# Attention in front of a feed-forward block: scores and sums in row tiles, one transpose a pair, masks added by VectorE, and another order of the first chunk

## The chip, the core and the metric

The kernel runs on one core of one Trainium2 chip. The metric is the device time of one execution in microseconds (us). The core's engines, as the profile calls them, are TensorE (PE; its weight loads PEld), VectorE (DVE), ScalarE (ACT), GpSimd (POOL) and SyncE (SP), which here only issues DMAs. Each engine works through its own queue in program order.

## The reference

Attention over 8 batches of 8 heads, 576 positions, 64 elements a head, with one of two masks, and a feed-forward block on its output. Cut to what matters:

```python
scores = (1 / np.sqrt(64)) * np.matmul(q, k.transpose(0, 1, 3, 2))
rel = pos[:, None] - pos[None, :]
mask_local = (rel >= 0) & (rel < 32)
mask_strided = (rel >= 0) & (pos[None, :] % 32 == pos[:, None] % 32)
# heads 0-3 take mask_local, heads 4-7 mask_strided; the rest is -1e9
attn = np.exp(scores - np.max(scores, axis=-1, keepdims=True))
attn = attn / (np.sum(attn, axis=-1, keepdims=True) + 1e-09)
x = np.matmul(attn, v)                      # regrouped: 4608 tokens x 512
h = x @ w_in                                # 512 x 2048
g = np.maximum(h, 0.0) + np.log1p(np.exp(-np.abs(h)))
out = g @ w_out                             # 2048 x 512
```

All of it is f32. A query of a local head sees only the 32 keys up to its own. For strided heads the host sorts positions by their remainder, so that a query sees only keys of its own group of 18; both masks then need no more than a window of 64 keys for a block of 32 queries.

## The kernel before, in words

**Pairs and blocks.** Heads go in pairs, 4 pairs a batch, 32 in all; pair n is of batch n // 4, and the two heads of a pair fill the 128 partitions of q and k (64 each). The 18 blocks of 32 queries of a pair are held as 9 chunks at two places, so that scores fill 128 partitions (place, head, query) and 9 x 64 columns.

**Scores** (`scores`, L355): q is laid out by `lay_out_q` (L264) as blocks of 64 columns, both heads side by side, with the other head's half of the rows set to zero (`zeros`, L222). One matmul of 128 rows by 64 columns then gives both heads of one block: 18 a pair, alternately for the upper and the lower 64 partitions of the output. In batches 0 and 1 TensorE also adds the mask, through an identity matrix (L340); from batch 2 on VectorE does (`add_mask`, L416).

**Softmax.** Maxima, either a subtraction with one wide exponential or nine exponentials with a bias, sums, `guard`, reciprocal, `normalize` (L389 to L447). In batches 0 and 1 these go by parts of six and three chunks straight from PSUM, from batch 2 on by whole rows of 576 columns (`row_maxima` L421, `row_subtract` L425, `row_exp` L431, `row_sums` L435).

**Transpose.** The probabilities must be turned for the sums: in batch 0 by TensorE against an identity (`early_transposes`, L477, L495) with copies out of PSUM (`early_copy`), later by 16 VectorE transposes of 32 partitions (`prob_transposes`, L457).

**Sums** (`weighted`, L525): 12 matmuls a pair, 128 keys by 64 columns of v, 96 queries each, in two halves of six; `v` is loaded in overlapping pieces (L293, L300). `x_part` splits the result into a high part (ScalarE, L563) and a low part (VectorE, L561).

**Feed-forward.** Tokens go in 9 chunks of 512, the hidden units in 16 blocks f. `hidden` (L629) has 12 matmuls of 512 columns a block, `output` (L669) 12; in between the softplus on ScalarE (L641 to L646) and VectorE (L650), and the split into high and low part (L264, L662). The weights come as 64-bit numbers and are turned into high and low parts in `w_scaled`, `w_shift` (L593), `w_last` (L600), `w_high`, `w_low` (L615).

**Order.** Batches 0 and 1 and chunk 0 follow the table `FIRST`, written out by hand; `ON_POOL`, `ON_VECTOR` and `ON_SCALAR` say which engine takes a step. In it `S` are scores, `X` maxima, `E` exponentials, `M` normalization, `P` or `T` transposes, `V` sums, `H` and `L` the parts of x, `F` and `O` hidden and output blocks (`Fa` is all but the last quarter of one). Everything later is placed by `Plan`, a list scheduler with costs per step: each pair's scores go between two blocks, in one group with the sums of the pair before (`work`, the joint group), one pair for every four steps of F and O.

## Time and profile before

| what | value |
|---|---|
| three runs | 891.38, 892.63, 892.89 us (median 892.63) |
| span of the profiled execution, first to last instruction | 890.1 us |
| DVE, ACT, POOL busy in the first 20 us | 15.2, 14.8, 14.0 us |
| transposes on VectorE (448) | 137 us busy |
| q's layout on ScalarE from pair 4 on (56 copies) | 71 us busy |

The profile is of one execution. A time of its own isn't given for that one; its span is 2.5 us below the median of the runs, for what lies before the first and behind the last instruction. A row of a group reads: line, engine, operation, output <- input, partitions x elements, count, then busy us and mean ns of one, then idle time of the engine just before. Matmuls overlap, so their means are longer than the distance from one to the next; a distance is read from starts in the timeline.

### The profile page before, as it was taken

The numbers are of one execution on the slowest core, as the hardware profiler recorded it, in microseconds if no ns is written. First come the engines' busy times: TensorE is split into PE (matmuls) and PEld (weight loads), VectorE is DVE, ScalarE is ACT, GpSimd is POOL, SyncE is SP. The second block draws the span as 40 slices with busy tenths as digits, with TensorE's granted clock in tenths as the row PEclk, the third lists the DMA queues.
The fourth block names the chain that finished last, engine by engine and source line by source line (L and its number), as shares of the span: only waits on it lengthen the run. The fifth ranks groups of instructions, "written<-read, shape, count | busy, mean of one in ns | idle before, by whom it ended". The sixth has DMA issues, their size and how long they took to land.

```text
span 890.1 us, 14332 instructions
## 1 busy us (share of the span) xinstructions
PE 879.0 (99%) x5634; PEld 723.6 (81%) x5634; DVE 576.6 (65%) x1268; ACT 445.8 (50%) x796; POOL 64.0 (7%) x93
## 2 busy tenths in 40 slices
PE   7999999999999999999999999999999999999998
PEld 5778888888888888888888888888888888888886
DVE  7878877788766777776766676677777333333332
ACT  7999665554544445445445454445543333333332
POOL 7254350000000000000000000000000000000000
PEclk9999999999999999999999999999999999999999
DMA  9856202121211122111211121111200010001001
GB/s 337 314 205 209 93 18 76 56 75 45 91 37 30 36 74 62 44 45 32 92 44 45 44 92 30 30 43 54 81 18 18 1 48 1 0 1 48 1 1 48
DMA packets 50083, 58.27 MB, mean 65 GB/s; under 512 B 3168, under 2 KB 35296, under 8 KB 50016
## 3 DMA queue, kind: packets, MB, share of 16 engines
q1 hardware_dynamic: 49728, 57.03, 19.5%
q8 instruction: 44, 0.72, 0.3%
q10 hardware_dynamic: 288, 0.33, 0.1%
q14 instruction: 23, 0.19, 0.1%
HBM read 47.91 MB, written 9.44 MB: 64 GB/s over the span
## 4 chain that ended last, share of the span: by engine, by line
PE 96%; ACT 2%; DMA 1%; DVE 1%; issue 0%; ACTq 0%
PE py L669 44%; PE ph L629 44%; PE ps L355 3%; PE pv L525 2%; PE po L525 1%; PE po L355 1%; DMA kT<-in_qk_dram 1%; PE idle L692 0%; ACT early_l L399 0%; ACT early_h L264 0%; ACT a_i L589 0%; ACT x_h L563 0%; ACT early_l L264 0%; PE py L355 0%; PE ps L340 0%
## 5 line engine op out<-in xcount | busy, mean ns | idle before, releaser
L669 PE MATMUL py<-w_o,gh 128*128 128x512 f32 x1152 | 358.4, 392 | 0.0
L629 PE MATMUL ph<-x_h,w_i 128*128 128x512 f32 x1152 | 355.5, 390 | 0.0
L641 ACT ACTIVATE u<-ph 128x512 f32<-128x512 f32 x144 | 86.3, 599 | 399.0 <-PE ph L629 398.6
L629 PEld LDWEIGHTS ph<-x_h,w_i 128*128 128x128 f32 x1152 | 215.7, 188 | 45.2
L669 PEld LDWEIGHTS py<-w_o,gh 128*128 128x128 f32 x1152 | 213.9, 188 | 46.4
L669 PE MATMUL py<-w_o,gl 128*128 128x512 f32 x576 | 224.1, 389 | 0.0
L629 PE MATMUL ph<-x_l,w_i 128*128 128x512 f32 x576 | 224.1, 389 | 0.0
L650 DVE SCALAR_TENSOR_TENSOR u<-ph,u 128x512 f32<-128x512 f32 x144 | 99.3, 690 | 178.3 <-ACT u L646 176.3
L457 DVE STREAM_TRANSPOSE pt<-prob 32x192 f32<-32x192 f32 x448 | 137.1, 314 | 6.4
L669 PEld LDWEIGHTS py<-w_o,gl 128*128 128x128 f32 x576 | 108.1, 188 | 22.8
L629 PEld LDWEIGHTS ph<-x_l,w_i 128*128 128x128 f32 x576 | 108.2, 188 | 22.6
L662 DVE TENSOR_TENSOR gl<-u,gh 128x512 fp32r<-128x512 f32 x136 | 94.3, 694 | 12.8 <-ACT gh L264 2.2
L644 ACT ACTIVATE u<-u 128x512 f32<-128x512 f32 x144 | 91.3, 634 | 4.3
L646 ACT ACTIVATE u<-u 128x512 f32<-128x512 f32 x144 | 91.1, 633 | 4.4
L264 ACT COPY qT<-prob 64x576 f32<-64x576 f32 x56 | 70.6, 1261 | 0.3
L264 DVE CAST gh<-u 128x512 fp32r<-128x512 f32 x128 | 54.5, 426 | 10.9 <-DVE u L650 0.5
L416 DVE TENSOR_TENSOR prob<-ps,mask_b 128x384 f32<-128x384 f32 x24 | 13.4, 558 | 50.0 <-PE ps L355 50.0
L355 PEld LDWEIGHTS ps<-kT,qT 128*64 128x64 f32 x720 | 24.0, 137 | 9.0 <-issue 8.5
L355 PE MATMUL ps<-kT,qT 128*64 128x64 f32 x720 | 27.6, 225 | 0.3 <-DMA kT<-in_qk_dram 0.3
L561 DVE TENSOR_TENSOR x_l<-pv,x_h 128x288 fp32r<-128x288 f32 (+2 forms) x47 | 18.8, 412 | 9.0 <-ACT x_h L563 8.9
L447 DVE TENSOR_TENSOR prob<-prob,st 128x576 f32<-128x576 f32 x27 | 21.9, 811 | 0.9
L525 PE MATMUL pv<-pt,v_in 128*64 128x96 f32 x396 | 22.1, 248 | 0.0
(100 smaller groups left out, 481.7 us busy)
## 6 DMA issues: line engine op xcount, KB each, us to landing
v_in<-in_v_dram SPq DMA_DIRECT2D x28, 320.0 KB, 3.5
out_dram<-o SPq DMA_DIRECT2D x35, 256.0 KB, 2.2
ri<-in_moe_w_in_dram SPq DMA_DIRECT2D x16, 512.0 KB, 7.3
ro<-in_moe_w_out_dram SPq DMA_DIRECT2D x16, 512.0 KB, 7.7
kT<-in_qk_dram SPq DMA_DIRECT2D x28, 288.0 KB, 2.9
prob<-in_qk_dram SPq DMA_DIRECT2D x28, 288.0 KB, 2.7
v_in<-in_v_dram SPq DMA_DIRECT2D x28, 48.0 KB, 2.7
room<-in_v_dram SPq DMA_DIRECT2D x4, 320.0 KB, 6.6
```

The source lines that it names most:

```text
L264: (engine.copy if engine is nc.scalar else engine.tensor_copy)(dst, src)
L355: nc.tensor.matmul(ps[rows[place], 64 * (x - lo) : 64 * (x - lo) + 64], lhsT=blocks_of(n)[:, c // 32].rearrange("p h l -> p (h l)"), rhs=k ...
L447: engine.tensor_tensor(pv, pv, rc.unsqueeze(2).broadcast_to(pv.shape), op=ALU.mult)
L457: nc.vector.transpose(pt[32 * (i + c) : 32 * (i + c) + 32, h, a : a + hi - lo, 32 * i : 32 * i + 32,], src[:, lo:hi, 32 * c : 32 * c + 32],)
L525: nc.tensor.matmul(po[64 * h : 64 * h + 64, TILE * x : TILE * x + TILE], lhsT=vs[n][:, a, h, :], rhs=pt_of(n, a)[:, h, a % 2], start=True, ...
L629: nc.tensor.matmul(ph, lhsT=w32["i", f][:, half, cc * P : (cc + 1) * P], rhs=x_of(x, cc)[:, t0 : t0 + n], start=(i == 0), stop=(i == 3 * N ...
L641: nc.scalar.activation(us[c, f], phs[c, f], AF.Abs)
L644: nc.scalar.activation(u, u, AF.Exp, scale=-1.0)
L646: nc.scalar.activation(u, u, AF.Ln, bias=1.0)
L650: nc.vector.scalar_tensor_tensor(u, in0=phs.pop((c, f)), scalar=0.0, in1=u, op0=ALU.max, op1=ALU.add)
L662: engine.tensor_tensor(g, us.pop((c, f)), ghs[c, f].bitcast(F32), op=ALU.subtract)
L669: nc.tensor.matmul(py[t], lhsT=g[:, sl], rhs=w32["o", f][:, half], start=(f == 0 and n == 0), stop=(f == NFC - 1 and n == 2),)
```

## The change

Seven things change together.

1. **Scores** become 36 matmuls a pair: 64 rows (one head), 32 columns of q, 64 keys. Head h and half `half` of the blocks write 32 partitions each. q needs no zeros and one copy for both heads.
2. **The blocks** are numbered in halves: chunk x of half 0 is block x, of half 1 block 9 + x.
3. **Masks** are added by VectorE in all batches; softmax goes by whole rows everywhere. The strided mask is held in full (15 x 64 columns instead of 12 x 64), loaded in three DMAs on SP's queue instead of one on ScalarE's.
4. **Transpose**: one VectorE transpose of 128 x 576, block by block, for each pair, in batch 0 too. The TensorE transposes, their copies, identities and cleared pads are gone.
5. **Sums** become 38 matmuls a pair: 32 keys (rows) of one head and half, 64 columns of v, 64 queries (32 at the ends), each result added up from two neighbouring windows. Half 0 goes to one PSUM bank, half 1 to another, alternately.
6. **v** comes in four loads a pair, one for each half and head, instead of two for both heads.
7. **The table `FIRST`** is a new one, with batch 1's sums in one group with the next scores (`J`), and with other steps on GpSimd and VectorE. In `Plan` the costs of S, Q and P are other numbers.

```diff
 def scores(n, part):
...
-        for x in range(lo, hi):
-            for place in range(2):
-                a, i = block_at(x, place)
-                c = TILE * a + 32 * i
-                nc.tensor.matmul(
-                    ps[rows[place], 64 * (x - lo) : 64 * (x - lo) + 64],
-                    lhsT=blocks_of(n)[:, c // 32].rearrange("p h l -> p (h l)"),
-                    rhs=k_of(n)[:, c : c + 64],
-                    start=not masked or n == 0 and x == lo,
-                    stop=not masked or n > 0 and x == hi - 1,
-                )
+        for x in range(lo, hi):
+            for half in range(2):
+                for h in range(2):
+                    c = 32 * (NCHK * half + x)
+                    to = 64 * half + 32 * h
+                    nc.tensor.matmul(
+                        ps[to : to + 32, 64 * (x - lo) : 64 * (x - lo) + 64],
+                        lhsT=q_of(n)[64 * h : 64 * h + 64, c : c + 32],
+                        rhs=k_of(n)[64 * h : 64 * h + 64, c : c + 64],
+                        start=True,
+                        stop=True,
+                    )
...
+    def prob_transposes(n):
+        nc.vector.transpose(pt_of(n), flat_prob(n))
+
+    def weighted(n, joint=False):
+
+        if joint:
+            banks = shared[n + 1], ps_h.tile([P, 512], F32, tag="ph", name=f"pv_{n}")
+        elif n == 1:
+            banks = [ps_h.tile([P, 512], F32, tag="ph", name=f"pv_{n}_{i}") for i in range(2)]
+        else:
+            taken.append(n)
+            banks = (
+                ps_o.tile([P, 512], F32, tag="po", name=f"pv_{n}_0"),
+                ps_s.tile([P, 512], F32, tag="ps", name=f"pv_{n}_1"),
             )
+        pos[n, 0], pos[n, 1] = banks
+        for j in [*range(1, NCHK + 1, 2), *range(0, NCHK + 1, 2)]:
+            lo, hi = max(j - 1, 0), min(j + 1, NCHK)
+            first = 64 * j - 32 if j else 0
+            for half in range(2):
+                if half == 0 and j == 0:
+                    continue
+                for h in range(2):
+                    at = 64 * half + 32 * h
                     nc.tensor.matmul(
+                        banks[half][64 * h : 64 * h + 64, 32 * lo : 32 * hi],
+                        lhsT=vs[n][at : at + 32, j],
+                        rhs=pt_of(n)[at : at + 32, first : first + 32 * (hi - lo)],
+                        start=(j == 1),
+                        stop=(j == NCHK - 1),
+                        skip_group_check=True,
                     )
...
+    def lay_out_q(n, engine=nc.scalar):
+
+        to = q_of(n).rearrange("p (m l) -> p m l", l=32)
+        copy_on(engine, to, raws[n].rearrange("p (l m) -> p m l", l=32))
...
+        for half in range(2):
+            j = 1 - half
+            for h in range(2):
+                part = src[(HALF - 32) * half : HALF + HALF * half, h * D : h * D + D]
+                rows = slice(64 * half + 32 * h, 64 * half + 32 * h + 32)
+                nc.sync.dma_start(t[rows, j:], part.rearrange("(j k) d -> k j d", k=32))
...
 ON_POOL = """
-D10 D20 x10 D31 hi0 x21 r2 x31 r3 hi3 hi1 ho1 Gh0 ho2 x41 hi4 r4 x50 x51 x60 Gh6 x61 r6 ho8 ho10
+D0 s0 s1 D3 r0 r1 s3 hi4 hi3 ho4 s4 ho5 Gh5 r4 ho2 Gh2 s5 ho9 hi11 hi10 hi14 hi13 Gh6 Gh10 s7 hi15
...
-WIDE = """
-00 11 20 30
+ROWS = """
+0 2
 """.split()
...
-        cost = 1.3
+        cost = 0.8
         if joint(i):
-            cost = 2.5
+            cost = 1.6
```

**TensorE, a joint group.** On TensorE, between the hidden block of one step and the output block of another, a pair's joint group stood like this in the steady stage before (`ps` and `po` take scores, `po` and `pv` sums; a matmul's size is rows of output by columns):

```order
L629 MATMUL ph_10_3077<-x_l_612,w_i_930 128x512
L355 MATMUL ps_0_3094<-kT_101,qT 64x64 x12
L355 MATMUL po_3107<-kT_101,qT 64x64 x6
L525 MATMUL po_3107<-pt,v_in 64x96 x6
L525 MATMUL pv_3120<-pt,v_in 64x96 x6
L669 MATMUL py_104<-w_o_1313,gh_8_3056 128x512 x2
```

In the changed kernel the beginning of the same group, and the first of its sums:

```order
L495 MATMUL ph_11_2433<-x_l_607,w_i_1302 128x512
L297 MATMUL ps_0_2450<-kT_101,qT 32x64 x24
L297 MATMUL po_2475<-kT_101,qT 32x64 x12
L390 MATMUL po_2475<-pt,v_in 64x64 x2
L390 MATMUL pv_2488<-pt,v_in 64x64 x2
L390 MATMUL po_2475<-pt,v_in 64x64 x2
L390 MATMUL pv_2488<-pt,v_in 64x64 x2
```

The place of the group is the same; inside it 18 score matmuls are now 36 and 12 sums 38, and the two banks of the sums alternate, so that neither half is complete before the end.

**VectorE, the start.** On VectorE the softmax of the first two pairs stood so before (`early_l_91` and `early_l_93` hold the probabilities of pairs 0 and 1, `st` their maxima and sums, `py` the scores in PSUM):

```order
L389 TENSOR_REDUCE st_181<-py_104 128x6
L376 TENSOR_TENSOR early_l_91<-py_104,st_181 128x6x64
L389 TENSOR_REDUCE st_181<-py_105 128x3
L393 TENSOR_SCALAR st_181<-st_181 128x3
L385 TENSOR_REDUCE st_181<-early_l_91 128x6
L389 TENSOR_REDUCE st_209<-py_107 128x3
```

And in the changed kernel, up to the third pair's first mask:

```order
L316 TENSOR_TENSOR early_l_93<-py_107,mask_b 128x192
L321 TENSOR_REDUCE st_244<-early_l_93 128x9
L316 TENSOR_TENSOR early_l_95<-py_105,mask_b 128x192
L459 TENSOR_SCALAR a_i_251<-a_i_251 128x512
L316 TENSOR_TENSOR early_l_95<-py_104,mask_b 128x384
L352 TENSOR_REDUCE st_158<-early_l_91 128x9
L321 TENSOR_REDUCE st_249<-early_l_95 128x9
```

VectorE's queue now has two mask additions and one reduction over nine chunks for each pair where it had reductions by parts; the subtraction of pair 0 and all normalizations of batch 0 have gone to GpSimd's queue.

**SP, the loads.** SP's queue for the same time; before, from the first v on (`room` takes v, `early_l` k, `ri` a block of the first weights):

```order
L293 DMA room_109<-in_v_dram 96x128
L300 DMA room_109<-in_v_dram 128x5x128
L282 DMA early_l_97<-in_qk_dram 128x576
L569 DMA ri_368<-in_moe_w_in_dram 128x4x128
L569 DMA ri_394<-in_moe_w_in_dram 128x4x128
L293 DMA room_110<-in_v_dram 96x128
```

And now:

```order
L256 DMA room_109<-in_v_dram 32x9x64 x2
L256 DMA room_109<-in_v_dram 32x10x64 x2
L243 DMA early_l_97<-in_qk_dram 128x576
L435 DMA ri_281<-in_moe_w_in_dram 128x4x128
L435 DMA ri_284<-in_moe_w_in_dram 128x4x128
L256 DMA room_108<-in_v_dram 32x9x64 x2
```

Each v takes four issues; four blocks of the first weights are asked for ahead of the last v, and a first block of the second weights (`ro`) only behind it.

380 lines of the change are left out of this document (112 added, 268 removed).

## The prediction

> **What bounds the kernel now.** The page comes first: its busy shares and its chain.
>
> ```profile
> span 890.1 us, 14332 instructions
> PE 879.0 (99%) x5634; PEld 723.6 (81%) x5634; DVE 576.6 (65%) x1268; ACT 445.8 (50%) x796; POOL 64.0 (7%) x93
> ```
>
> TensorE (PE) is busy 99% of the span, the next engine 65%. So an edit counts by what it does to TensorE's queue, or to the time at which that queue can start. The windows show where TensorE isn't full: I cut the span at the first feed-forward matmul (30.44), at the first score group after chunk 0 (139.66) and at the last sums (697.07).
>
> ```profile
> 0.00:30.44 30.44, 23.49 (x482) 18.29 (x483) 24.21 (x52) 24.39 (x67) 19.18 (x46) 1.00 0.90 309
> 30.44:139.66 109.22, 108.97 (x679) 87.44 (x677) 86.10 (x186) 89.39 (x205) 44.86 (x47) 1.00 0.46 158
> 139.66:697.07 557.41, 557.41 (x3625) 461.50 (x3625) 400.43 (x920) 264.38 (x414) 0.00 (x0) 1.00 0.16 51
> ```
>
> Columns: length, then busy time of PE, PEld, DVE, ACT, POOL, then clock, DMA share, GB/s. Only the front has gaps on TensorE; there VectorE, ScalarE (24 of 30 us each) and the loads (share 0.90) are near full. From 30.44 on nothing but TensorE's own work counts. How much of that is attention, not feed-forward, follows from the dense matmuls, L629 (first two rows) and L669.
>
> ```profile
> 30.44:139.66 109.22, 55.46 (x228) 42.25 (x228) 1.00 0.46 158
> 139.66:697.07 557.41, 265.15 (x1105) 207.28 (x1104) 1.00 0.16 51
> 30.44:139.66 109.22, 46.83 (x192) 35.66 (x192) 1.00 0.46 158
> 139.66:697.07 557.41, 268.32 (x1104) 205.41 (x1104) 1.00 0.16 51
> ```
>
> From the chain of waits, the price of one dense matmul; from the windows, four steps with one pair in them:
>
> ```profile
> 280.75 2.72 PE py L669 x12
> ```
>
> ```profile
> 264.21:288.38 24.17, 24.17 (x158) 20.02 (x157) 16.73 (x38) 11.24 (x18) 0.00 (x0) 1.00 0.14 41
> ```
>
> 12 in 2.72 us are 0.2267 us each. Chunk 0's stage: 420 x 0.2267 = 95.2, so 14.0 of its 109.2 us are the attention of batch 1. Steady stage: four steps are 8 x 2.72 = 21.76, so a **joint group** (scores of one pair, sums of the pair before) costs 24.17 - 21.76 = 2.41 us; 23 of them and one score group alone fill what the 2209 dense matmuls leave of 557.4. The timeline shows one from inside.
>
> ```profile
> 285.81 0.39 PE L629 MATMUL ph<-x_l,w_i 128*128 128x512 f32 x1
> 286.12 0.92 PE L355 MATMUL ps<-kT,qT 128*64 128x64 f32 x24
> 286.87 0.52 PE L355 MATMUL po<-kT,qT 128*64 128x64 f32 x12
> 287.22 0.67 PE L525 MATMUL po<-pt,v_in 128*64 128x96 f32 x12
> 287.72 0.67 PE L525 MATMUL pv<-pt,v_in 128*64 128x96 f32 x12
> 288.31 0.73 PE L669 MATMUL py<-w_o,gh 128*128 128x512 f32 x2
> ```
>
> A matmul on plain f32 leaves two records here (24 for 12 in the program), its two passes. 12 score passes take 287.22 - 286.87 = 0.35, so two take 58 ns; 12 sums passes take 0.50, so two take 83 ns. Scores are 18 x 58 = 1.05 us, sums 12 x 83 = 1.00. The last dense matmul is through at 285.81 + 0.23 = 286.04; 1.05 later would be 287.09, but the sums start at 287.22: **entering** the small tiles costs 0.13. The rest, 2.41 - 2.05 - 0.13 = 0.23, is spent on **leaving** them.
>
> Do two small tiles really run side by side? Batch 0's mask matmuls say so:
>
> ```profile
> 6.57 0.48 PE L355 MATMUL py<-early_l,early_h 128*64 128x64 f32 x6
> 6.88 0.33 PE L340 MATMUL py<-mask_b,ident_b 128*64 128x384 bf16 x2
> 7.04 0.34 PE L355 MATMUL py<-early_l,early_h 128*64 128x64 f32 x6
> ```
>
> Two of 384 columns are through in 0.16 us, and one alone, at the dense rate, needs 384/512 x 0.227 = 0.17. So two column tiles overlap fully. Two f32 passes in 58 ns then mean 58 ns per tile.
>
> **Steady stage, 23 joint groups.** The change makes 36 score matmuls of 32 rows of output on four tiles and 38 sums on four tiles: 148 passes for 60. If four tiles overlap as two do, a tile has 18 score passes, 18 x 58 = 1.05 as before. In the sums the busiest tile has 20 passes: 16 of 64 columns, 16 x 58 = 0.93, and four of 32 columns, at between 29 and 58, taken at 44: 0.17. Together 1.10 for 1.00. Scores and sums no longer have one tile shape, so a change of shape is added between them; the trace has none between two small shapes, so between 0 and 0.23, taken at the entering 0.13, to which it is most alike. That gives 0.23 a group, **+5.3 us** (ends +1 and +9). The Trainium skill, "TensorEngine Tiling (Array Packing)", Tiling Modes, says that any change of tiling mode drains TensorE; by it the addition would be due, and the 0.23 at 285.81 and 288.31 agrees for the shapes that this trace has.
>
> The transposes, q's layout and the masks of later batches cost nothing on this path:
>
> ```profile
> L457 DVE STREAM_TRANSPOSE pt<-prob 32x192 f32<-32x192 f32 x224 | 82.8, 370 | 3.9
> L416 DVE TENSOR_TENSOR prob<-ps,mask_b 128x384 f32<-128x384 f32 x24 | 13.4, 558 | 50.0 <-PE ps L355 50.0
> L416 DVE TENSOR_TENSOR prob<-po,mask_b 128x192 f32<-128x192 f32 x24 | 8.6, 358 | 19.3 <-ACT x_h L563 19.3
> L425 DVE TENSOR_TENSOR prob<-prob,st 128x576 f32<-128x576 f32 x24 | 18.0, 750 | 0.0
> L421 DVE TENSOR_REDUCE st<-prob 128x9 f32<-128x576 f32 x24 | 17.9, 745 | 0.0
> L447 DVE TENSOR_TENSOR prob<-prob,st 128x576 f32<-128x576 f32 x27 | 21.9, 811 | 0.9
> ```
>
> 16 transposes of 32 rows become one of 128 x 576; three of 192 columns would be 1.1 us, the other passes over 576 columns are 0.75 to 0.81, and I take 0.8. VectorE loses some 4 us a pair, but it is idle 28% of that stage and TensorE not at all. This is hidden already; it buys nothing.
>
> **Chunk 0's stage.** Gone are four mask matmuls a pair and the separate score and sum groups; left are a score group (2.15 - 1.10 + 0.36 = 1.41), three joint ones (2.15 + 0.49 = 2.64) and one sums group (1.10 + 0.36 = 1.46): 10.8 for 14.0, **-3.2 us** (-5 to 0). What is late next there is ScalarE, busy 89 of 109 us; it loses a half of q's layout per pair.
>
> **The front.** Batch 0 loses its mask matmuls, the TensorE transposes and their twelve copies; it gains two mask additions a pair and puts two of the four layouts of q, a subtraction and all normalizations on GpSimd. Its end now:
>
> ```profile
> 29.79 0.72 PE L525 MATMUL pv<-early_l,room 128*64 128x96 f32 x12 [0.50 <-DVE x_l L561]
> 30.44 0.73 PE L629 MATMUL ph<-x_h,w_i 128*128 128x512 f32 x2
> ```
>
> F0, the first feed-forward block, needs all four pairs and ends at 30.44 + 2.9 = 33.3. Rows for the new chain:
>
> ```profile
> L431 ACT ACTIVATE prob<-prob 128x576 f32<-128x576 f32 x24 | 16.5, 688 | 9.2 <-DVE prob L425 9.1
> L561 DVE TENSOR_TENSOR x_l<-pv,x_h 128x288 fp32r<-128x288 f32 x35 | 15.7, 451 | 9.0 <-ACT x_h L563 8.9
> L563 ACT CAST x_h<-pv 128x288 fp32r<-128x288 f32 x35 | 13.8, 398 | 8.7 <-PE pv L525 8.6
> L600 DVE SCALAR_TENSOR_TENSOR a_i<-ri,a_i 128x512 uint32<-128x512 uint32 x16 | 11.2, 705 | 0.2
> L264 POOL COPY early_h<-raw_q 64x576 f32<-64x576 f32 x3 | 3.7, 1239 | 0.7 <-DMA raw_q<-in_qk_dram 0.7
> L447 POOL TENSOR_TENSOR early_l<-early_l,st 128x576 f32<-128x576 f32 x2 | 2.6, 1308 | 1.4 <-DVE st L443 1.2 <-ACT early_l L264 0.2
> ```
>
> ```profile
> 9.71 0.31 ACT L399 ACTIVATE early_l<-py,st 128x64 f32<-128x64 f32 x1 [0.75 <-DVE st L393]
> 10.02 0.30 ACT L399 ACTIVATE early_l<-py,st 128x64 f32<-128x64 f32 x1
> ```
>
> Nine exponentials follow each other every 0.3 us: 2.7 a pair. Laying each engine's new queue out with these, 0.1 us between engines: pair 0's q is laid out by 5.7, masked by 8.0, its maxima done at 8.7, subtracted on GpSimd until 10.0, exponentials until 10.7. ScalarE goes on with pair 1's (13.4), pair 2's (15.2, after VectorE's subtraction at 14.4), weights, pair 3's (16.4 to 19.0). GpSimd normalizes four times, 1.3 each, the last until 22.1; VectorE transposes pairs 2, 1 and 3 until 23.3; TensorE's last sums end at 25.3, their high parts at 26.1, the low parts, behind three weight steps on VectorE, at 28.0. F0 ends at 28.7 instead of 33.3: **-4.6 us** (-8 to 0). What is late next is GpSimd's row of normalizations and the loads:
>
> ```profile
> raw_q<-in_qk_dram SPq DMA_DIRECT2D x4, 288.0 KB, 4.8
> room<-in_v_dram SPq DMA_DIRECT2D x4, 320.0 KB, 6.6
> ```
>
> Each v is now four loads instead of two, and up to pair 3's v the queue holds 8 x 288 KB of q and k, one more q, four weights of 512 KB, four v and the masks: 6.3 MB, 20.3 us at 309 GB/s and then some to land, against sums of pair 3 at 24.
>
> **Sum**: -4.6 - 3.2 + 5.3 + 0.1 (two more sums groups' passes at the very end) = -2.4 against the profiled execution, whose span is 890.1. The three runs' median is 892.63, 2.5 above the span for what lies around it; so 892.6 - 2.4 = **890.2**.
>
> **Rivals.** (a) *Four tiles don't overlap.* Head 0 and head 1 sit in different row tiles and write the same bank. If tiles of different rows take turns there, scores and sums double: (1.05 + 1.10) x 27 pairs = +58, **948**: slower. The trace has only tiles with all rows, so nothing speaks on it; the two column tiles that overlapped in one bank speak against. The Trainium skill, "TensorEngine Tiling (Array Packing)", Restrictions and Gotchas, says that different row tiles cannot use one PSUM bank at the same time, which is this rival; no run here shows it yet.
>
> (b) *TensorE can't be fed so fast.* 60 passes in 2.19 us, 36 ns each, is what the trace keeps up over a group; 148 in 2.15 would be 15 ns. At 25, half way, a group has 3.7 us: +1.55 x 27 = +42, **932**. It ends slower than before from 16 ns on. The Trainium skill, "TensorE: Matmul & The Clock Gate", "Wait — 56ns, not 53.3ns?", has a floor of about 25 ns from the start of one matmul to that of the next, which would be about this price; the trace, with two passes of different tiles in 58 ns, stays above that floor and cannot tell.
>
> (c) *Row tiles make a pass cheaper.* A dense pass does 64 columns in 28 ns, a bf16 pair too; only two f32 passes side by side take 58. If that is their common reading of 128 rows at 4 bytes, the sums, whose tiles share no row, halve: -0.55 x 27 = -15, **875**; the scores as well: **861**. For it: all three rates fit. Against: two passes per matmul fit as well with f32 itself at half rate.
>
> (d) *The front doesn't shorten*, held by loads or by GpSimd: -2.4 + 4.6, **895**, from 4 us of delay on.
>
> **How the numbers follow.** Forecast 0.44, (a) 0.09, (b) 0.10, (c) 0.24, (d) 0.13. The forecast's own range is 884 to 897. The range of 862 to 912 leaves out (a), most of (b) and the end of (c), about 0.2. This kernel's measurement can tell about 0.2%, 1.8 us. Faster: 0.26 of the forecast, (c) 0.24, (d) 0.04, 0.54. Same: 0.10 + 0.06 = 0.16. Slower: 0.08 + 0.09 + 0.10 + 0.03 = 0.30.
>
> **What would show it.** In the timeline of a joint group: score passes in 1.05 us and sums in 1.1 (right), 2.1 each (a), an even spacing of all passes above 15 ns (b), 0.55 (c); a gap of some 0.13 between the two. F0 complete near 28.7; the dense matmuls of chunk 0's stage plus 10.8 us. I am wrong if the period of four steps isn't near 24.40, or if TensorE has idle time after F0.

## The result, and where the time went

The changed kernel takes 917.2 us (median of 4 runs, 915.97 to 918.57), the kernel before 892.0 in the same comparison (890.47 to 892.89): a ratio of 1.0284, with a 95% interval of 1.0267 to 1.0301. It is slower by 25 us, where 2.4 us less was forecast, and it lies above the forecast's whole range of 862 to 912. The profiled execution has a span of 914.2 us for 890.1.

The page of the changed kernel, its first lines, then from its list of queues (packets, MB, share of 16 engines) the one that brings instructions:

```profile
span 914.2 us, 19113 instructions
PE 896.8 (98%) x8202; PEld 730.0 (80%) x8202; DVE 473.2 (52%) x863; ACT 401.4 (44%) x748; POOL 52.0 (6%) x62
q8 instruction: 64, 1.05, 0.5%
```

VectorE and ScalarE lost work (577 to 473, 446 to 401 us), VectorE some 4 us a pair as forecast, and TensorE is as full as it was. So the 24 us must be found on TensorE's queue. The windows of the changed kernel, cut at the same events as in the prediction (first feed-forward matmul, first score group after chunk 0, last sums), and the four steps of one joint group; the columns are those of the prediction's windows:

```profile
0.00:36.30 36.30, 22.43 (x602) 18.17 (x603) 20.34 (x42) 18.64 (x57) 13.19 (x24) 0.67 0.90 244
36.30:144.16 107.86, 107.86 (x1013) 87.54 (x1012) 85.75 (x152) 79.13 (x191) 38.86 (x38) 1.00 0.51 159
144.16:717.48 573.32, 573.31 (x5686) 467.32 (x5685) 301.44 (x560) 236.30 (x391) 0.00 (x0) 1.00 0.17 47
717.48:914.20 196.72, 193.18 (x905) 156.92 (x904) 65.72 (x110) 67.35 (x111) 0.00 (x0) 1.00 0.05 17
269.81:294.67 24.86, 24.86 (x245) 20.27 (x244) 12.61 (x23) 10.01 (x16) 0.00 (x0) 1.00 0.15 38
```

Against the stages of before (30.44, 109.22, 557.41, and 890.1 - 697.07 = 193.0) that is +5.9, -1.4, +15.9 and +3.7, together +24.1. The last of these is the strange one: once the last sums are done there is no attention left, only the same 828 feed-forward matmuls, and the stage costs 3.7 us more. The chain of waits shows it at every block. Before, and after, far from any attention:

```profile
736.63 2.72 PE py L669 x12
739.35 2.72 PE ph L629 x12
```

```profile
741.24 2.80 PE py L535 x12
744.04 2.76 PE ph L495 x12
```

Twelve dense matmuls take 2.72 us before, whichever block it is, far from small tiles; after the change mostly 2.76 in a hidden block and 2.80 in an output block. There are 144 of each: 144 x (0.04 + 0.08) = 17 us by these rounded rows; by the starts of the matmuls themselves (2.758 and 2.796) it is 16.4. That takes the usual block for every block. Added up one by one, the distances from each dense matmul behind F0, the first feed-forward block, to the next matmul on TensorE are 802.1 us here and 787.7 in e1 below, where the price is the old one: the term is 14.4 us. The granted clock is 1.00 in both, and the instructions are the same. Nothing in the forecast's sum had this term: it took the 0.2267 us of a dense matmul as given.

The other surprise is the front, which grew from 30.44 to 36.30 us. Its granted clock is 0.67 where it was 1.00, and its loads ran at 244 GB/s where it was 309. The joint groups, which the prediction feared most, look like this in the timeline:

```profile
269.49 0.39 PE L495 MATMUL ph<-x_l,w_i 128*128 128x512 f32 x1
269.81 0.87 PE L297 MATMUL ps<-kT,qT 64*32 64x64 f32 x48
270.50 0.52 PE L297 MATMUL po<-kT,qT 64*32 64x64 f32 x24
270.94 0.27 PE L390 MATMUL po<-pt,v_in 32*64 32x64 f32 x2
...
272.00 0.34 PE L390 MATMUL pv<-pt,v_in 32*64 32x64 f32 x6
272.27 0.72 PE L535 MATMUL py<-w_o,gh 128*128 128x512 f32 x2
```

48 score passes start within 270.50 - 269.81 = 0.69 us, 14.4 ns each: by their starts they come in fours, 6 to 7 ns apart, and the next four 56 ns after the first. So four tiles, two of them in other rows, work side by side at the pace of one. This is as forecast.

### The profile page after: what moved, and what is told of

The parts are those of the page before. It is cut to its first block, busy times and chain, and to the rows that moved or that the text cites. A ratio compares the mean times of both kernels' runs of the same rounds, so it can differ in the third digit from the quotient of the medians.

```text
span 914.2 us, 19113 instructions
## 1 busy us (share of the span) xinstructions
PE 896.8 (98%) x8202; PEld 730.0 (80%) x8202; DVE 473.2 (52%) x863; ACT 401.4 (44%) x748; POOL 52.0 (6%) x62
## 3 DMA queue, kind: packets, MB, share of 16 engines
q8 instruction: 64, 1.05, 0.5%
HBM read 45.86 MB, written 9.44 MB: 60 GB/s over the span
## 4 chain that ended last, share of the span: by engine, by line
PE 97%; DMA 2%; SPq 1%; DVE 0%; issue 0%; ACT 0%
PE py L535 45%; PE ph L495 44%; PE pv L390 3%; PE po L390 3%; PE ps L297 2%; PE po L297 1%; DMA early_l<-in_qk_dram 1%; DMA room<-in_v_dram 1%; SPq L231 0%; SPq L435 0%; SPq L270 0%; ACT x_h L429 0%; DVE x_l L427 0%; SPq L256 0%; SPq L243 0%
## 5 line engine op out<-in xcount | busy, mean ns | idle before, releaser
L535 PE MATMUL py<-w_o,gh 128*128 128x512 f32 x1152 | 364.8, 398 | 0.0
L535 PE MATMUL py<-w_o,gl 128*128 128x512 f32 x576 | 227.1, 394 | 0.0
L390 PE MATMUL pv<-pt,v_in 32*64 32x64 f32 (+1 forms) x1192 | 38.8, 220 | 0.0
L234 ACT COPY qT<-prob 128x576 f32<-128x576 f32 x28 | 36.1, 1289 | 0.0
L390 PEld LDWEIGHTS pv<-pt,v_in 32*64 32x64 f32 x1192 | 34.9, 133 | 0.7 <-DVE a_o L466 0.4
L348 ACT ACTIVATE prob<-prob 128x576 f32<-128x576 f32 x24 | 16.5, 686 | 39.1 <-DVE prob L325 39.1
L390 PE MATMUL po<-pt,v_in 32*64 32x64 f32 (+1 forms) x936 | 32.9, 220 | 0.0
L390 PEld LDWEIGHTS po<-pt,v_in 32*64 32x64 f32 x936 | 29.3, 133 | 2.4
L316 DVE TENSOR_TENSOR prob<-po,mask_b 128x192 f32<-128x192 f32 x28 | 10.0, 357 | 35.6 <-ACT x_h L429 33.8
```

The source lines that it names most:

```text
L234: (engine.copy if engine is nc.scalar else engine.tensor_copy)(dst, src)
L316: nc.vector.tensor_tensor(pv, sv, mask_of(n, j), op=ALU.add)
L348: nc.scalar.activation(pv, pv, AF.Exp, scale=SCALE)
L390: nc.tensor.matmul(banks[half][64 * h : 64 * h + 64, 32 * lo : 32 * hi], lhsT=vs[n][at : at + 32, j], rhs=pt_of(n)[at : at + 32, first : f ...
L535: nc.tensor.matmul(py[t], lhsT=g[:, sl], rhs=w32["o", f][:, half], start=(f == 0 and n == 0), stop=(f == NFC - 1 and n == 2),)
```

## Experiments on the dense matmuls

**Theory.** The new attention tiles are smaller (transposed probabilities and q 2304 instead of 4608 bytes per partition, v 2560 instead of 3072, and no identity; only the mask grew, from 1536 to 1920), so all that is laid out behind them moved. In the built programs, per partition:

```
                before   after
g (gh, gl)         256     256     (1 x 256)
x (h, l)         36096   31104     141 x 256        121 x 256 + 128
w_i of block 0  113920  108928     445 x 256        425 x 256 + 128
u               216960  211968
```

**All addresses as before** (e1), against rivals in other work or in the order:

```diff
     prob_all = const.tile([P, 2 * S], F32, name="prob")
+    pad = const.tile([P, 1248], F32, name="pad")
+    nc.gpsimd.memset(pad[:, :1], 0.0)
```

> The changed kernel with one unused tile of 4992 bytes per partition behind the attention's tiles, so that x, the weights, st, u and io lie at the same SBUF addresses as in the kernel before (x from 36096, w_i of block 0 from 113920, u from 216960); nothing else moves. Theory P (placement: the dense matmuls cost 231.3 ns instead of 226.7 because the smaller attention tiles moved their operands to other addresses): twelve dense matmuls fall from 2.76 and 2.80 to 2.72 us, 3456 x 4.6 ns = 16 us go, about 901. Rival N (no placement: other work of VectorE and ScalarE, or the order of the instructions, slows them): they stay at 2.76 and 2.80, about 917.

Measured: 903.4 us, ratio 1.013 (1.0113 to 1.0147). The chain of waits of this run:

```profile
760.62 2.72 PE ph L497 x12
763.34 2.72 PE py L537 x12
```

Every block far from small tiles is back at 2.72, and 13.8 us of the 25 are gone, with one unused tile. Placement is shown. The span of the profiled execution fell by 13.9 us, 9.4 of it in the steady stage and 3.7 behind the last sums; the front and chunk 0's stage together gained 0.8. Chunk 0 behind F0 gained 1.2 (from 39.04 to 144.16 in the changed kernel, from 39.48 to 143.39 here), and F0 itself lost: it begins 0.8 earlier, but at half the clock for part of its time, and takes 3.94 us instead of 2.74. So much can the clock do to a single execution of the front.

**128 bytes are enough** (e2): the same edit with a tile of 32 numbers.

> The same with 128 bytes instead of 4992: x and the weights move from 384 to 0 above a multiple of 512, u and io from 0 to 128. Theory A (alignment of the dense operands: what counts is that x and w start on a multiple of 256, as they do in the kernel before, 256 above a multiple of 512): 2.72 per twelve, about 901. Rival B (the exact addresses count, as a distance between what TensorE reads and what VectorE and ScalarE write): somewhere between 2.70 and 2.85, not 2.72 in both blocks. Rival N: 917.

Measured: 904.51 us, ratio 1.0138 (1.0118 to 1.0158), all blocks at 2.72. x and w now lie at other addresses than before, but on multiples of 256. The distances of the dense matmuls behind F0 add up to 787.8 us, as in e1. (In the profiled execution F0 is complete only at 42.71, for 39.04 in the changed kernel; more on that below.)

**u and io alone** (e4): the 128 bytes stand between st and u, so that x and w stay where the change put them.

> The changed kernel with 128 unused bytes between st and u: x and the weights stay where the change put them (384 above a multiple of 512), u and io move from 0 to 128. Theory A: nothing moves, 2.76 and 2.80 per twelve, about 917. Theory U (u's and io's place against the operands counts, the tiles that VectorE and ScalarE write beside the matmuls): towards 2.72, down to 901.

Measured: 918.98 us, ratio 1.03 (1.028 to 1.0321), blocks at 2.76 and 2.80. Where the tiles lie that VectorE and ScalarE write beside the matmuls doesn't matter for the price.

**One of two operands** (g1 and h2). In a hidden block w_i is loaded into TensorE and x streams through; in an output block gh or gl is loaded (they lie on a multiple of 256 in every kernel here) and w_o streams. In g1, 128 bytes ahead of x and 128 more between x and w align x alone; in h2, 128 bytes between x and w align w alone.

> The changed kernel with 128 unused bytes ahead of x and 128 more between x and the weights: x starts on a multiple of 256, the weights 128 above one. In hidden blocks x is what streams through TensorE and w_i what is loaded into it; in output blocks w_o streams and gh, gl (always on a multiple of 256) are loaded. Theory R (what streams must start on a multiple of 256): hidden blocks 2.72 us, output blocks 2.80, about 909. Rival L (the loaded operand counts): hidden blocks 2.76, output blocks 2.72. Rival both: 2.74 to 2.76 and 2.80, 915.

> The changed kernel with 128 unused bytes between x and the weights: the weights start on a multiple of 256, x 128 above one; gh and gl on a multiple of 256 as always. So far, twelve matmuls: all aligned 2.72; x and w both 128 off 2.76 (hidden), w 128 off and g aligned 2.80 (output), w 128 off and x aligned 2.80 (hidden). Theory W (the weights' place alone sets the price): 2.72 in both blocks, about 901. Theory D (it is the difference between what is loaded and what streams that counts): output blocks 2.72, hidden blocks 2.76 to 2.80, about 906 to 908.

Measured: 924.54 us and 917.65 us (one run each). From the chains of waits, first g1, then h2:

```profile
751.43 2.80 PE ph L499 x12
754.22 2.80 PE py L539 x12
```

```profile
751.98 2.79 PE ph L498 x12
754.77 2.73 PE py L538 x12
```

The table that comes out, with what each operand is off a multiple of 256:

```
loaded  streams   twelve matmuls
   0       0         2.72          before, e1, e2 (both blocks)
 128     128         2.76          after, e4, hidden
   0     128         2.80          after, e4, g1, output
 128       0         2.80          g1, hidden
   0     128         2.79          h2, hidden (w_i loaded)
   0       0         2.73          h2, output
```

In g1 both single theories fell, and "both" was near for output blocks alone. In h2 theory W fell, and theory D (the difference between what is loaded and what streams) came near for both blocks. Its total of 906 to 908 was too low even so: 144 hidden blocks at 0.07 us more are 10 us on top of e2's 904.5.

Against theory D stands the third row, where both are 128 off and a block still takes 2.76. The starts inside the blocks settle it. Here are the eleven distances between the twelve matmuls of one block, in ns, read from the starts in the traces (the block's own start behind its name); a full pace is 226 and 227 in turn:

```
loaded streams  block                              distances
   0      0     before 505.87, behind small tiles  337 236 228 233 231 226 227 227 226 227 227
   0      0     h2 529.61, output behind hidden    231 233 231 226 227 227 226 227 227 226 227
 128    128     after 529.39, hidden behind output 236 224 231 236 228 232 231 227 227 226 227
 128    128     after 45.86, hidden behind hidden  227 227 226 227 227 226 227 227 226 227 227
   0    128     after 532.14, output behind hidden 241 233 231 231 229 230 232 241 232 231 232
   0    128     h2 532.35, hidden behind output    234 224 237 230 237 229 238 229 237 230 237
```

The fourth of these blocks in the timeline of the changed kernel, its first and its last row:

```profile
45.86 0.62 PE L495 MATMUL ph<-x_h,w_i 128*128 128x512 f32 x2
...
48.35 0.40 PE L495 MATMUL ph<-x_l,w_i 128*128 128x512 f32 x1
```

Eleven distances in 48.35 - 45.86 = 2.49 us are 226 ns each, with both operands 128 off. All six hidden blocks of the changed kernel that directly follow a hidden block are like this one, and so are the six of e4 and the six of e5. So the full pace doesn't ask for multiples of 256. It comes where the two operands are equally far off one: there the distances fall to 227 within seven matmuls, after whatever disturbed them. Where the two differ by 128 they stay uneven, at some 233 on average. The 2.76 of a hidden block is what the output block ahead of it leaves behind, and it isn't always left: the block right behind the last sums ran at the old pace, though an output block stood ahead of it.

```profile
721.85 2.73 PE ph L495 x12
```

That is theory D, and it fits every row. Why a difference costs time, and why it takes several matmuls to settle, is open: a clash of the next weight load with the stream, whose timing is carried from matmul to matmul, would fit, but no run shows it. Only offsets of 0 and 128 were tried. By theory D, moving gh and gl by 128 bytes would do as well as moving x and w; no run tried that.

The Trainium skill, "SBUF — State Buffer", Operand start alignment, asks only that an operand starts on a multiple of its element size, which all of these do; for the time, these runs ask for more. The same page, SBUF: two separate sides, says that TensorE's port waits for no other engine; e4, with 2.76 and 2.80 wherever the others write, is in keeping with that.

## Experiments on the front

The prediction had laid out the front from durations, 0.1 us between engines. Rows of the changed kernel's timeline for three of its steps, and the chain of waits:

```profile
10.69 0.82 DVE L316 TENSOR_TENSOR early_l<-py,mask_b 128x192 f32<-128x192 f32 x2 [9.57 <-DMA mask_b<-in_masks_dram]
13.78 0.67 ACT L348 ACTIVATE early_l<-early_l 128x576 f32<-128x576 f32 x1
27.57 1.15 POOL L364 TENSOR_TENSOR early_l<-early_l,st 128x576 f32<-128x576 f32 x1 [2.01 <-DVE st L360]
```

```profile
6.64 7.45 DMA early_l<-in_qk_dram
16.23 6.95 DMA room<-in_v_dram
28.16 6.52 PE pv L390 x184
36.30 5.62 PE ph L495 x24
```

Pair 0 is masked from 10.69 (it was to be done by 8.0), exponentiated at 13.78 (10.0), the last normalization ends at 28.72 (22.1), the last sums at 34.7 (25.3), F0 at 36.30 + 2.74 = 39.0 (28.7). The lag grows along the whole front; loads stand in the chain twice, and the last three sums take 6.52 us, where three at the 1.33 of the joint group above (270.94 to 272.27) would be 4.0. So there were four theories: the clock, v's sixteen small loads, the masks' loads, and the order of the queues.

**The clock** (e5). It is halved in the middle of the changed kernel's front, as in this window of 3 us (length, busy TensorE, then clock, DMA share, GB/s):

```profile
18.00:21.00 3.00, 1.92 (x72) 0.50 1.25 252
```

```diff
-q2 q0 k0 D0 W S01 mask1 q1 mask0 k1 wi0 Y01 S00 Y00 X0
+q2 q0 k0 D0 W S01 mask1 q1 mask0 k1 wi0 Y01 S00 W0 Y00 X0
...
+    for i, n in enumerate((16, 4, 12, 8, 6)):
+        task(f"W{i}", dummies, n)
```

> The changed kernel with 46 dummy matmuls of 128x512 in the five gaps of TensorE's front (16 after the first pair's scores, then 4, 12, 8 and 6), which leave the granted clock no idle time to fall in. Theory C (the front is long because TensorE, idle in it, runs at a granted clock of 0.50 from 12 to 34 us: scores of a pair 2.15 to 2.30 us for 1.14, the last three sums 6.51 for 3.96): clock 1.00 in the front, the last three sums in 4.0 us, the first dense matmul at 33 to 33.8 instead of 36.30, time 914. Rival L (the loads and the queue on VectorE set the front, and a faster TensorE only waits longer): first dense matmul after 35.5, time 916 to 917.

Measured: 918.25 us, ratio 1.0292 (1.0272 to 1.0313). The front's clock is 0.92 instead of 0.67, and the first dense matmul starts at 37.20, not earlier: theory C fell, and rival L stands. With TensorE kept busy the clock stays up, so the halved clock comes from the waiting; what it costs the sums lies beside other waits.

For F0 itself the clock's price can be read. F0 in the changed kernel, then in e2 (columns of the first windows, the clock third from the end):

```profile
36.30:39.04 2.74, 2.74 (x12) 2.25 (x12) 2.19 (x4) 0.66 (x2) 0.00 (x0) 1.00 1.06 387
```

```profile
37.63:42.71 5.08, 5.08 (x12) 3.92 (x12) 0.93 (x2) 0.00 (x0) 0.00 (x0) 0.50 1.04 403
```

The runs from here on have the 128 unused bytes of e2, so 904.5 us is their base. One profiled execution of a front is a weak witness: in the six whose front has the same steps and loads (changed kernel, e1, e2, e4, g1, h2), F0 is complete at 39.0, 39.5, 42.7, 42.6, 41.3 and 43.0. A difference of less than four us there tells nothing by itself.

**v in one load per pair**, in pieces of 256 bytes as before (f1) and of 2560 bytes (f2). In both, v is laid out accordingly in memory ahead of the launch, with one unused block:

```diff
-        for half in range(2):
-            j = 1 - half
-            for h in range(2):
...
-                nc.sync.dma_start(t[rows, j:], part.rearrange("(j k) d -> k j d", k=32))
+        nc.sync.dma_start(t, src.rearrange("j p d -> p j d"))           # f1
+        nc.sync.dma_start(t, src.rearrange("p (j d) -> p j d", d=D))    # f2
```

> The changed kernel with the 128 unused bytes (dense matmuls at 2.72 per twelve), and each pair's v laid out in memory so that it comes in one load instead of four, still in pieces of 256 bytes, 320 KB with the unused ones. Theory Q (the front is late because 16 loads of v hold SP's queue and the semaphores of the loads in flight: v's last piece was asked for at 27.1 and landed at 28.9): v of the last pair in by 25, first dense matmul 3 us earlier than 36 to 38, time 901. Rival S (the 256-byte pieces themselves are slow: 210 to 250 GB/s for 309): v no earlier than 27.5, time 904.

> As the run before, but with v laid out so that each partition's 2560 bytes stand together. Theory Q: no different from the run before, 901. Theory S (small pieces): the rate in the front goes back to about 310 GB/s, v of the last pair in by 24, first dense matmul at 32 to 33, time 900. If neither helps (rival E: VectorE's queue and GpSimd's normalizations hold the front), first dense matmul at 35.5 or later, 903.

Measured: 902.42 us, ratio 1.0126 (1.0096 to 1.0155), and 902.65, 1.0128 (1.0099 to 1.0158). The last landing of v that the trace has is at 23.37 and 23.02, for 28.11 in e2, so theory S fell: pieces of 256 bytes don't hold v up. F0's first matmul comes at 32.3 and 33.5, for 37.6 in e2, but its second only at 35.96 and 36.36, and F0 is complete at 39.5 and 38.9. Five us in the loads are at most some 2 in the time, and these can't be told from nothing: the intervals overlap e2's (1.0118 to 1.0158). The size of the pieces made no difference that can be told.

**The local mask first** (f3), and that with v in whole rows (f4):

```diff
-q2 q0 k0 D0 W S01 mask1 q1 mask0 k1
+q2 q0 k0 mask0 D0 W S01 q1 mask1 k1
```

> The changed kernel with the 128 unused bytes, and the local mask (which pair 0 needs) asked for right behind pair 0's q and k, ahead of the strided mask and pair 2's q. Theory M (the front's chain starts late, because VectorE's first addition waits at 10.69 for that mask, landed at 10.59): the first addition at 7 to 7.5, the first sums 2 to 3 us earlier, the first dense matmul 2 us earlier if the loads behind let it, time 902. Rival Q/S (v and the loads set the end of the front): first addition earlier, first dense matmul no earlier, 904.5.

> Both: the local mask first and v in one load of whole rows. If the two delays stand one behind the other, first dense matmul at 30 to 31 and time 898 to 899; if only one of them is on the path, as in the better of the two runs before.

Measured: 901.6 us, ratio 1.0117 (1.0081 to 1.0152), and 902.98, 1.0132 (1.0103 to 1.0161). VectorE's first addition comes at 6.5, four microseconds earlier, but its third, the first of the next pair, at 12.97 and 13.04, for 12.89 in e2, and F0 is complete at 40.1 and 40.2. The sum of the two delays fell: the first dense matmul was to come at 30 to 31 and came at 33.8 in f4, the second at 36.3. Theory M alone is open. Its time of 902 us came, 2.9 below e2's median, but the intervals overlap, and F0's end lies inside the spread above.

**The strided mask in one load** (f5). The queue of SyncE in f4 shows why the next pair didn't follow (start, length, what is issued):

```profile
2.57 0.43 SPq L233 DMA_DIRECT2D raw_q<-in_qk_dram  x1
3.04 1.24 SPq L267 DMA_DIRECT2D mask_b<-in_masks_dram  x2
4.33 2.81 SPq L245 DMA_DIRECT2D early_l<-in_qk_dram  x1
```

The change loads the strided mask in two loads whose source repeats 64 rows for the second head. Behind them the next issue takes 2.81 us instead of 0.43. In f5 the mask lies in memory for all 128 rows:

```diff
-        for place, lo, hi, at in ((0, 6, 12, 6), (1, 6, 9, 12)):
...
-            src = bass.AP(tensor=src.tensor, offset=src.offset, ap=[[0, 2], *src.ap])
-            nc.sync.dma_start(mask_b[:, 64 * at : 64 * (at + hi - lo)], src)
+        nc.sync.dma_start(mask_b[:, 6 * 64 :], masks[:, 6 * 64 :])
```

> As the run with the local mask first and v whole, but with the strided mask laid out for all 128 rows in memory, so that it comes in one plain load instead of two that repeat 64 rows. In the traces so far, the loads stand nearly still for 2.5 us behind those two (5 to 80 GB/s at 5.5 to 8 us), and the next load's issue takes 2.8 us instead of 0.4. Theory K (that stall starts the chain late): k of the second pair lands at 8.5 instead of 11.35 and the first block of w_in at 10 instead of 12.62, and F0 is complete 2 to 3 us earlier than the 40.16 there, 900. Rival O (the order of the queues on VectorE, ScalarE and GpSimd sets the front): F0 complete at 39 or later, 902 to 903.

Measured: 900.38 us, ratio 1.0093 (1.0073 to 1.0113), below e2's interval; its two runs (899.5, 901.25) lie below both of f4's (902.38, 903.58). k of the second pair lands at 7.65 instead of 11.35, VectorE's third addition comes at 8.71 instead of 13.04, and F0 is complete at 36.73 instead of 40.16: 3.4 us earlier in the profiled executions, 2.6 by the medians. Theory K stands. The same queue in f5 goes on without a stop:

```profile
3.04 0.43 SPq L263 DMA_DIRECT2D mask_b<-in_masks_dram  x1
3.52 0.43 SPq L245 DMA_DIRECT2D early_l<-in_qk_dram  x1
```

In windows of 1 us, with the columns of the first windows (the last three are clock, DMA share, GB/s), the 16 DMA engines are almost idle in f4 (a share of 0.10) where f5 has them full (0.99); f4 first, then f5:

```profile
6.00:7.00 1.00, 1.00 (x72) 0.94 (x70) 0.36 (x1) 0.24 (x1) 0.00 (x0) 1.00 0.10 23
```

```profile
6.00:7.00 1.00, 0.90 (x65) 0.74 (x54) 0.39 (x2) 0.56 (x1) 0.00 (x0) 1.00 0.99 371
```

The Trainium skill, "DMA: Bandwidth & Descriptors", Rules for kernel authors, says that a leading broadcast of c copies keeps a whole transfer on at most c of the engines. With the two copies here that would be 2 of 16, a share of 0.125; the 0.10 of f4 agrees. Which engines carried these loads the trace doesn't show one by one.

**Another order** (f6): f5 with its table of steps rearranged, so that no step waits in its queue ahead of one that is ready, and other steps on GpSimd. The first row of the table and the front's part of GpSimd's list:

```diff
-q2 q0 k0 mask0 D0 W S01 q1 mask1 k1 wi0 Y01 S00 Y00 X0 k2 D2 q3 v1 D1 k3 S10 S11 S21 Y10 Y11 s0 X1
+W wi0 q0 k0 D0 mask0 q1 S01 Y01 k1 D1 mask1 S00 q2 k2 q3 Y00 S10 ai0 D2 X0 Y10 S11 s0 Y11 k3 S20
...
-D0 s0 s1 D3 r0 r1 s3
+M0 M2 M3 hi0 hi1 hi4 s0 s2 s3 r0
```

> The run before, with the front's table of steps and engines in another order: no step of ScalarE or VectorE stands in its queue behind a load or a result that comes later than the next pair's step (E0 ahead of the first weights, Z0 ahead of pair 2's masks, all q loads ahead of the weights). Theory O: exponentials of pair 0 at 10 instead of 13.2, sums of the last pair done by 29 to 30 instead of 35, F0 complete at 33 to 35, 896 to 897. Rival B (the front is bound by what VectorE, ScalarE and GpSimd have to do in it, whatever the order): F0 complete at 38 or later, 901 or more.

Measured: 903.52 us, ratio 1.0129 (1.0112 to 1.0146), slower than f5, with F0 complete at 41.3. Theory O fell, and the timeline of TensorE in this run shows why the earlier sums (17.93 for 20.16 in f5) bought nothing:

```profile
17.93 1.76 PE L384 MATMUL pv<-early_h,room 32*64 32x64 f32 x50 [1.16 <-DVE early_h L361]
21.60 1.01 PE L384 MATMUL pv<-early_h,room 32*64 32x64 f32 x26 [1.92 <-issue]
24.81 3.05 PE L384 MATMUL pv<-early_h,room 32*64 32x64 f32 x101 [2.19 <-issue]
30.86 3.90 PE L384 MATMUL pv<-early_h,room 32*64 32x64 f32 x127 [3.00 <-issue]
```

In brackets stands the idle time ahead and what ended it; "issue" is nothing that the trace shows. TensorE stops in the middle of a group of sums. Each matmul pass is two instructions on TensorE, a load and a multiplication. Counted so, from TensorE's first, these stops stand at:

```
instruction           442    696    950   1204     (stop in us, between starts)
f6                   2.27   2.23   3.31   2.48
f5, instruction       444                 1206
                     2.32   none   none   2.41
before               none at any of these places
```

They are 254 apart, with a record missing here and there. The queue named "instruction" on the page brought 64 packets, 1.05 MB: 16384 bytes each, 256 instructions if one has 64 bytes. And 64 x 256 = 16384 is nearly what TensorE ran, 2 x 8202 = 16404; before it was 44 packets for 2 x 5634, and in e5, with 46 more passes, 65. A packet of that queue arrives in or near every stop. Not every such place has a stop: f5 has none at 696 and 950. The last stop of f6 ends, by the trace, with a block of weights from GpSimd, so it may be that wait. And the stop ahead of 24.81, at instruction 748, is not at such a place; what it waited for is open.

**The stops follow the count** (h1): f5 with 2 dummies at the start instead of 10, 16 instructions fewer.

```diff
-    first["W"] = lambda: dummies(10)
+    first["W"] = lambda: dummies(2)
```

> As the run with the strided mask in one load, but with 2 dummy matmuls at the start instead of 10, so 16 instructions fewer stand on TensorE ahead of the first feed-forward block. In the runs so far TensorE stands still for 2.2 to 3.6 us, waiting for nothing that the trace names, at instructions 442, 696, 950 and 1206 of its stream: 254 to 256 apart, and 256 instructions of 64 bytes are the 16384-byte pieces of the instruction queue, one of which arrives in each of these stops. Theory I (TensorE waits for its instructions at the ends of these pieces): the stop behind the first dense matmul (2.41 us at 30.36) moves eight dense matmuls into F0, where those already handed over cover most of it; F0 complete 1.5 to 2.4 us earlier than 36.73 there, 898.5. Rival X (the stop is a wait for x_l or for weights): it stays behind the first or second dense matmul, F0 complete at 36.5 or later, 900 to 901; the cold start (fewer dummies) may cost 0.5 in both.

Measured: 899.42 us, ratio 1.0083 (1.0062 to 1.0103), not to be told from f5. TensorE at F0's start, f5 and then h1:

```profile
30.36 0.50 PE L488 MATMUL ph<-x_h,w_i 128*128 128x512 f32 x1
32.77 0.58 PE L488 MATMUL ph<-x_h,w_i 128*128 128x512 f32 x1 [1.90 <-issue]
...
34.86 1.05 PE L488 MATMUL ph<-x_h,w_i 128*128 128x512 f32 x2
35.71 0.47 PE L488 MATMUL ph<-x_l,w_i 128*128 128x512 f32 x1
```

```profile
29.65 3.69 PE L383 MATMUL pv<-early_h,room 32*64 32x32 f32 x118 [2.61 <-issue]
33.27 0.74 PE L488 MATMUL ph<-x_h,w_i 128*128 128x512 f32 x2
```

The stop behind F0's first matmul is gone, so it was no wait for x_l or weights: rival X fell. At instruction 1206, now inside F0, 0.45 us are left of 2.41. But the piece before it now ends inside the last sums, at instruction 952, and there TensorE stops for 2.9 us where f5 had no stop. F0 is complete at 36.37 instead of 36.73, not the 1.5 us earlier that I expected. The first stop stands at instruction 443, as in f5 (444), although 16 instructions fewer lie ahead of the same matmul, while the stop at 748, which follows the program and not the count, is now at 732. So the stops that are counted off in 254s follow the count. That TensorE waits for its instructions there is the reading that fits; removing the wait wasn't done: the stop went to the next place where small passes run out of instructions. The rows of f5 show the clock's price again: behind the stop two dense matmuls take 35.71 - 34.86 = 0.85 us, twice the usual.

In the changed kernel itself the pauses of 1.6 us at 16.2 and 1.85 at 34.4 lie at instructions 452 and 1204, near or at such places, but the trace has other waits that end there (a load of k, x_l). Whether the instructions held it as well isn't shown. The Trainium skill, "Runtime: NRT & Kernel Launch", Instruction fetch mechanics, has blocks of 256 instructions, fetched ahead and mostly hidden. The count agrees (64 packets of 16384 bytes for 16404 instructions). In dense work the fetch is hidden here too; among small passes it was not always: 2.23 and 3.31 us at two ends of blocks in f6.

## One part of the change alone

Chunk 0's stage was the one that got shorter. h3 is the kernel before with batch 1 alone done as the later batches: masks by VectorE, scores and sums in joint groups of the old tile shapes, the same addresses and front.

```diff
-        masked = b < 2
+        masked = b < 1
...
-        elif b == 1 or part == 0:
+        elif part == 0:
...
+    def joint_scores(n):
+        scores(n, 0)
+        scores(n, 1)
+        if n > NPAIR:
+            for half in range(2):
+                weighted(n - 1, half, True)
```

> The kernel before, with batch 1 (the attention inside chunk 0) done as the later batches are there: masks added by VectorE instead of by TensorE, and a pair's scores and the sums of the pair before in one group; same tiles, layouts, loads, addresses and front. In the changed kernel this part of the change took chunk 0's attention from 14.0 to some 11 us. Theory J (that part of the change is worth its saving by itself): one score group, three joint groups of 2.41 and one of sums are 10.0 for 14.0 us, 888 to 889, faster than both. Rival V (VectorE and ScalarE, busy 86 and 89 of these 109 us, fall behind with the added mask steps and TensorE waits for them): 892 or more, with idle time on TensorE in chunk 0's stage.

Measured: 901.44 us, ratio 1.0101 (1.0084 to 1.0118): slower by 9.6. A window of it inside chunk 0, and the matmuls behind one joint group there:

```profile
60.00:80.00 20.00, 17.46 (x118) 14.41 (x114) 15.90 (x37) 16.59 (x42) 9.20 (x8) 0.91 0.53 181
```

```profile
64.47 0.73 PE L644 MATMUL ph<-x_h,w_i 128*128 128x512 f32 x2 [2.54 <-DVE x_l L576]
```

TensorE is busy for 109.2 us of the stage, as before (109.0), but the stage grew from 109.2 to 118.1 us: 8.9 are idle, 4.5 of them in three waits for VectorE's x_l behind a group. Rival V stands, for this order of steps. In the changed kernel the same regrouping paid. VectorE is as busy there as before (85.75 us for 86.10), ScalarE less (79.13 for 89.39), and the steps stand in another order; which of these made it pay isn't shown.

## Why the prediction was wrong, step by step

- **Four tiles overlap: right.** Rival (a) falls: passes of different row tiles start 7 ns apart into one bank, and four take 56 ns, not the 116 of two turns of 58. The Trainium skill's rule in "TensorEngine Tiling (Array Packing)", Restrictions and Gotchas, that they cannot use one PSUM bank at the same time, is not what this trace shows: neither the starts nor the time of a group are those of tiles that take turns. Rival (b) falls: 14.4 ns per pass are kept up within a group. Rival (c) falls: a pass became no cheaper.
- **The joint group: mechanism right, size nearly.** 0.23 us more was forecast. With the dense matmuls back at 2.72 (e1), the steady stage is

```profile
143.39:707.32 563.93, 563.93 (x5685) 466.70 (x5685) 301.52 (x560) 236.46 (x391) 0.00 (x0) 1.00 0.18 48
```

  against 557.41: 6.5 us for 23 groups, 0.28 each, for 5.3. Four steps with one pair take 24.45 us in e1, for the forecast's 24.40, and 24.86 in the changed kernel. The change of shape between scores and sums is there: 146 ns from the last score pass to the first of the sums, for 36 from the last pass of one four to the first of the next: 110 ns for the change, where 130 were taken.
- **The price of a dense matmul: the first step that failed.** The sum was made only of what the diff adds and removes; all 3456 feed-forward matmuls were taken at 0.2267 us. They cost 14.4 us more, since the smaller tiles moved x and the weights by an odd multiple of 128 bytes (e1, e2), and gh and gl not, so that in output blocks what is loaded and what streams no longer agreed. This term alone would have turned the sign: -2.4 + 14.4 = +12.0.
- **Chunk 0's stage: mechanism right, size nearly.** -3.2 was forecast. From F0's end to the stage's end it was 106.4 us before and is 105.1 now; with the dense matmuls at the old price (e1) it is 103.9, so -2.5 of attention. TensorE is busy for all of the 107.86 us there.
- **The front: the second step that failed.** For F0's end -4.6 was forecast, and +5.7 came (39.04 for 33.30). The step was to lay out each engine's queue from durations, "0.1 us between engines", and to hold the loads against their sum of bytes alone. Left out were when each load lands (the local mask at 10.59 and pair 3's v at 28.90, behind two mask loads that stop the queue), the clock that falls when TensorE waits (0.67 over the front), and perhaps the supply of instructions for passes of 15 ns. Rival (d) was the right direction; its "delay" was priced at 4.6 and measured 10.3 (39.0 for 28.7), which alone would have turned the sign too. Of this the strided mask's two loads are 2.6 to 3.4 (f5). The rest lies in waits beside each other, and what each of them costs stays open.
- **The tail: right** where the dense price is as before (193.0 in e1, for 193.0).
- **VectorE and ScalarE's savings buy nothing: right.** They have 103 and 44 us less work, and TensorE, busy for the whole steady stage before, is so after the change.

Added up, the span is 26.5 us longer than forecast (+24.1 for -2.4): the price of the dense matmuls 14.4, the front 10.3, the joint groups 1.2, chunk 0's attention 0.7, and the tail and rounding nothing that counts.

## What to carry to other kernels

When a change alters the size of any tile, look at where everything behind it now starts: here 128 bytes of padding were worth 13 us, more than any part of the change itself. Look at both operands of a matmul: what counted was whether they agree. Lay out a start-up phase by when loads land and by the order of each queue, not by the sum of durations. And when matmuls are split into smaller ones, count instructions as well as passes: half as much again on TensorE was hidden behind dense work, and in several runs not where only small passes ran.

## What the runs showed of the hardware that was not expected

- A dense matmul of 128x512 takes 226.7 ns when what is loaded and what streams start equally far off a multiple of 256 bytes of a partition (both 0 or both 128), and 233 on average when they differ by 128. After a difference, or after small tiles, the distances take up to seven matmuls to settle. No wait shows it; only the spacing of starts does.
- Two loads whose source repeats its rows, the copies outermost, held the loads behind them for some 2.4 us (an issue of 2.81 us for 0.43) at a tenth of the DMA engines' time, and cost 2.6 to 3.4 us at the end of the front.
- In f5, f6 and h1 TensorE stopped for 1.7 to 3.3 us at places that lie a multiple of some 254 instructions apart, among passes of small tiles and when the first dense matmuls begin. Not every such place has a stop, and beside dense matmuls only a rest of 0.45 us was seen (h1). That it waits there for the next piece of its instructions fits the count.
- The same 12 dense matmuls took 2.74 us at a granted clock of 1.00 and 5.08 at 0.50, and when the clock fell and rose in the front differed from one profiled execution to the next.
